# Order of tile conversions, k/v loads and stores at the end of the first unit's first stage

## The chip, the cores and the metric

The kernel runs on one core of a Trainium2 chip. The metric is the device time of one execution in microseconds (us). The core's engines each run their own instructions in order and wait for one another through semaphores. In the profile they are PE (TensorE, matrix products; PEld is its weight load), ACT (ScalarE), DVE (VectorE), POOL (GpSimd) and SP (SyncE, which here only issues transfers; its queue is shown as SPq). Transfers run on 16 DMA engines that all queues share.

## What is computed

A linear attention without softmax, normalized per head, followed by a feed-forward layer:

```python
kv = np.einsum('bhsd,bhse->bhde', k, v)
out = np.einsum('bhsd,bhde->bhse', q, kv)
rms = np.sqrt(np.mean(out * out, axis=-1, keepdims=True) + 1e-06)
x = (out / rms * g_norm).transpose(0, 2, 1, 3).reshape(4608, 512)
h = x @ w_in                      # (512, 2048)
g = s * np.maximum(h, 0.0) ** 2 + b
result = g @ w_out                # (2048, 512)
```

There are 8 batches of 8 heads, 576 positions and 64 columns per head. q, k, v and g_norm are float32; w_in and w_out are float64, and the chip has to turn them into float32 itself.

## The kernel before

**Units.** The 4608 rows are done in nine units of 512 rows. A unit has a first stage (x by w_in, then squared ReLU, scale s and offset b) and a second (by w_out). The first unit is special: during it the weights are loaded and converted.

**Products.** Most of both stages is computed by a scheme of seven products in place of eight (Strassen's, in Winograd's form), on halves of the operands. The products are called x1, z2, x6, y7, x5, x3 and y4: the letter is the PSUM tile (x_ps, z_ps, y_ps) that they go to, the digit the number of the product. x1, x6, x5 and x3 accumulate in one tile, and between them ScalarE copies the intermediate sum out: `keep("r1", ...)` behind x1, r2 behind x6, r4 behind x5 (line 718, shown as `r<-x_ps`). A product that continues in the tile must wait for the copy. The results are four tiles a11, a12, a21 and a22 for each of the four blocks s of the 2048 columns, and the sum s1 = a21 + a22.

In the first unit the blocks s = 0, 1, 2 are computed plainly (`mm1_plain`, twelve slots), and only the block s = 3 by seven products (`mm1`). Its x3 and y4 are put behind the first product of the second stage, x1(0), in the loop at line 1782. For a11, a12 and a22 VectorE adds the copy (line 250) and squares the ReLU (line 647), and `scale_g` later has ScalarE scale them (line 644). For a21 all of it is on ScalarE (lines 652, 653, 644).

**Weights.** w_in and w_out come in 16 tiles of 1 MB: tiles 0 to 7 are w_in, 8 to 11 the upper half of w_out (w_up), 12 to 15 the lower (w_dn). A tile is loaded into one of three buffers (tag "raw"). `raw(i)` is ScalarE's part of its conversion (lines 225 and 230, in place), `convert(i)` VectorE's (a shift, line 235, and an integer addition, line 245, into the final place); the end of convert(i) frees the buffer and sends the load of tile i + 3. `more(i)` subtracts halves of w_up for the seven products. When the tiles are through, the same three buffers take, in turn, k and v of batch 1, heads 0 to 3 (behind convert(13)), heads 4 to 7 (behind convert(14)), and a temporary (behind convert(15)).

**What the first unit also does.** `store_w2(1, 5)` writes two planes of w_up to DRAM, for the units after this one (four transfers on SP). `load_kv(1, i)` loads k and v (two transfers each on SP), `loads(1, half)` loads q for the second unit (four transfers each). `kv_product(1)` uses k and v in slot 6 of the second stage, and the attention for the second unit is spread over slots 7 to 13 as in `side_of`. Later stores (planes 3, 2, 6, 7 and 4) go out on the same queue; `t4` overwrites plane 2 of w_dn, and so waits for its store.

**Order.** The order of instructions on each engine is the order in which the program's lines are written. SP issues transfers in order too: one whose buffer is not free holds up all behind it. In `first_unit`, the loop over functions at line 1663 writes the order around x1 to x5; the loop at line 1782 that around the second stage.

Of the kernel before, what the change touches and what calls it, by code (L numbers as in the profile page):

```python
# [16 lines left out]
def kernel(  # L17
# [78 lines left out]
    def load_kv(b, i, pool, queues=(nc.sync,), **kw):  # L96

        t = pool.tile([P, 4 * R * D], U32, name="kv_sb", **kw)
        view = t.bitcast(FP32).rearrange("p (m l j d) -> p m l j d", m=2, l=2, j=R)
        for l in range(2):  # L100
            kv_in[b, 2 * i + l] = view[:, 0, l], view[:, 1, l]
        rows = P // len(queues)
        for m, src in enumerate((k, v)):
            flat = src[b, 4 * i : 4 * i + 4].rearrange("(l r) (p j) d -> (r p) l (j d)", l=2, j=R)
            for r, queue in enumerate(queues):
                at = slice(r * rows, r * rows + rows)
                queue.dma_start(
                    out=view[at, m].rearrange("p l j d -> p l (j d)"), in_=flat[at]
                )
# [73 lines left out]
    convp = tc.alloc_tile_pool(name="convp", bufs=1, side="right")  # L183
# [80 lines left out]
    def sums_w_in(s):  # L264
        ws[s] = wp.tile([P, 3, KH, 2, P], FP32, name=f"ws_{s}")
        a11, a12 = wa[s][:, :KH], wa[s][:, KH:]
        a21, a22 = wb[s][:, :KH], wb[s][:, KH:]
        s1, s2, s4 = (ws[s][:, i] for i in range(3))

        def s12():  # L270
            add(s1, a21, a22)
            sub(s2, s1, a11)

        def s34():
            sub(a21, a11, a21)
            sub(s4, a12, s2)

        return s12, s34
# [30 lines left out]
    def sub_w_out(i, a, b, steps=range(NS)):  # L309

        for s in steps:
            blocks = slice(2 * s, 2 * s + 2)
            sub(W2_AT[i][:, blocks], W2_AT[a][:, blocks], W2_AT[b][:, blocks])

    def store_w2(*which):
        for i in which:
            for q in range(2):
                nc.sync.dma_start(
                    out=w2_dram[i][:, q], in_=W2_AT[i][:, :, q * P : q * P + P]
                )  # L320
# [280 lines left out]
    def x_sums(u):  # L601
        b11, b12 = xT[u][:, :KH, :TB], xT[u][:, :KH, TB:]
        b21, b22 = xT[u][:, KH:, :TB], xT[u][:, KH:, TB:]

        def tiles(*which):
            for i in which:
                xs[u, i] = xp.tile([P, KH, TB], FP32, name=f"xs_{i}", tag=f"xs_{i}")

        def t12():
            tiles(5, 6)  # L610
            sub(xs[u, 5], b12, b11)
            sub(xs[u, 6], b22, xs[u, 5])

        def t34():
            tiles(7, 4)
            sub(xs[u, 7], b22, b12)
            sub(xs[u, 4], b21, xs[u, 6])

        return t12, t34
# [42 lines left out]
    def g_s1(s):  # L662
        add(ga["s1", s], ga["a21", s], ga["a22", s])
# [3 lines left out]
    def scale_g():  # L667
        while to_scale:
            affine(to_scale.pop(0))
# [831 lines left out]
    def hi(n, h=None):  # L1501
        fold_hi(blocks[n], h)

    def lo(n, h=None):
        round_lo(blocks[n], h)

    def shift(n, h=None):
        shift_hi(blocks[n], place(n), h)

    def plus(n, h=None):  # L1510
        add_lo(blocks[n], place(n), h)
        if h != 0:
            send_w()

    def more(n):

        s, lower = where(n)
        if n >= 2 * NS:
            if not lower:
                sub_w_out(5, 5, 1, [s])  # L1520
# [66 lines left out]
    def pairs_of(u):  # L1587
        return [attention_of_two(c) for c in (4 * u, 4 * u + 2)]
# [30 lines left out]
    def loads(u, i):  # L1619

        if u < U:
            for load in load_q(4 * u + 2 * i):
                load()  # L1623

    def raw(i):
        hi(i)
        lo(i)

    def convert(i):
        shift(i)  # L1630
        plus(i)

    def first_unit():
        of_x = x_sums(0)
        of_w = []

        for n, slot in enumerate(slots0):
            if n > 1:
                out_of = slot()
                if out_of:  # L1640
                    out_of()
                if n % 4 == 0:
                    g_s1(n // 4 - 1)
            if 0 < n < 9:
                raw(n + 2)
                convert(n + 2)
            elif n == 0:
                continue
            elif n == 9:
                of_w += sums_w_in(3)  # L1650
                of_w[0]()
            elif n == 10:
                of_x[0]()
                raw(11)
                of_x[1]()
            else:
                of_w[1]()
            if n < 11:
                scale_g()
            if n == 9:  # L1660
                more(8)
        a = mm1(0, NS - 1)
        for fn in (
            a["x1"], scale_g, partial(convert, 11), partial(more, 9),
            a["z2"], partial(raw, 12),
            a["x6"], scale_g, partial(g_s1, 2),
            a["y7"], partial(convert, 12),
            a["x5"], partial(raw, 13), scale_g, partial(more, 10), partial(more, 11),
        ):
            fn()  # L1670
        return a

    def x3(a):
        a["x3"]()

    def y4(a):
        for name in ("y4", "y4_square", "x3_s1", "x3_s3"):
            a[name]()
# [64 lines left out]
    for u in range(U):  # L1743
        A, B = pairs_of(u + 1) if u + 1 < U else (None, None)
        if u == 0:
            last = first_unit()
            second = mm2(0)
        else:
            if u == 1:
                loads(2, 0)  # L1750
                loads(2, 1)
            first, at_second = sides(u, A, B)
            if u > 1:
                run, last = mm1_deep(u)
                second = mm2(u, last, at_second)
                run(lambda n: [fn() for fn in first.get(n, [])], second["early"])
                second["rest"]()
                continue
            steps = [mm1(u, s) for s in range(NS)]
            second = mm2(u)  # L1760
        for s in range(NS if u > 0 else 0):
            a = steps[s]

            def at(n):
                for fn in first.get((s, n), []):
                    fn()

            at(0)
            a["x1"]()
            if s:  # L1770
                x3(steps[s - 1])
            a["z2"]()
            at(1)
            if s:
                y4(steps[s - 1])
            a["x6"]()
            at(2)
            a["y7"]()
            at(3)
            a["x5"]()  # L1780
        side = side_of(A, B, lambda: [fn() for fn in x_sums(u + 1)], u)
        for n, slot in enumerate(second):
            slot()
            if u == 0:
                if n == 0:
                    store_w2(1, 5)
                    for name in ("x3", "y4", "y4_square"):
                        last[name]()
                    convert(13)
                    scale_g()  # L1790
                    load_kv(1, 0, convp, tag="raw", bufs=3)
                    raw(14)
                    last["x3_s1"]()
                elif n == 1:
                    convert(14)
                    load_kv(1, 1, convp, tag="raw", bufs=3)
                    raw(15)
                    loads(1, 0)
                    loads(1, 1)
                elif n == 2:  # L1800
                    convert(15)
                    t2 = convp.tile([P, 4 * R * D], FP32, name="w_t2", tag="raw", bufs=3)
                    W2_AT[6] = t2[:, : FC // 2 * HN].rearrange("p (f n) -> p f n", n=HN)
                elif n == 4:
                    store_w2(3, 2)
                    sub_w_out(6, 3, 5)
                    store_w2(6)
            if n == 0 and u > 0:
                x3(steps[-1])
                y4(steps[-1])  # L1810
            for step in side.get(n, []):
                step()
        if u == 0:
            tc_late()
            pump()
# [30 lines left out]
```

## Time and profile before

| | us |
|---|---|
| median of 4 runs | 911.71 |
| lowest, highest | 910.71, 912.14 |
| the profiled execution | 911.80 |
| its span | 910.0 |
| TensorE busy | 897.2 |
| VectorE busy | 667.3 |
| ScalarE busy | 358.5 |

The granted clock of TensorE was 1.00 in the profiled execution. The span is the time from the first to the last instruction that the profile shows. A row of the timeline gives the start, the length, the engine, the source line, the operation, the tiles out<-in, and a count if rows were merged; in brackets stand the time in which the engine was idle before the row and what ended it. The queue's rows give the time SP took to issue a transfer, not the time until the data landed. The part of the span that the change touches lies between 70 and 95 us:

| us | DVE busy | ACT busy | DMA share | GB/s |
|---|---|---|---|---|
| 80 to 84 | 3.17 | 2.90 | 0.58 | 172 |
| 84 to 88 | 2.38 | 2.86 | 1.02 | 322 |
| 88 to 92 | 3.86 | 4.00 | 1.17 | 323 |
| 92 to 96 | 3.64 | 0.78 | 1.06 | 346 |

[...] PE is busy for the whole of each of these stretches.

### The profile page before, as it was taken

Reading aid. Unit: us, or ns where it says so; the run is one execution under the profiler, and the core shown is the slowest. Engines: PE = TensorE matmul, PEld = TensorE weight load, DVE = VectorE, ACT = ScalarE, POOL = GpSimd, SP = SyncE. Lnnn points to the kernel's source line nnn. Section 1 sums busy time; section 2 is a strip of 40 time slices with the busy share of each in tenths; the row PEclk is TensorE's granted clock in tenths of the full one; section 3 lists DMA queues with packets and bytes.
Section 4 is the critical chain, followed back from the end, with each engine's and each line's share of the span. In section 5 each row is a group of like instructions: output and inputs, shape, how many; then the busy total and the mean of one; then the engine's idle time right before and its main releaser. Section 6 shows DMA issues by size and latency. Waiting matters only on the chain.

```text
span 910.0 us, 19247 instructions
## 1 busy us (share of the span) xinstructions
PE 897.2 (99%) x7514; PEld 824.1 (91%) x7514; DVE 667.3 (73%) x1234; ACT 358.5 (39%) x603; POOL 228.3 (25%) x432
## 2 busy tenths in 40 slices
PE   7998999999999999999999999999999999999998
PEld 6887888888889998999889998999899989999998
DVE  2888677588557985887678857895878778874686
ACT  3877224531147115640366026701580057104710
POOL 2000016113624232810273035603440300021000
PEclk9999999999999999999999999999999999999999
DMA  9686957339953994379626973597439812891286
GB/s 260 221 291 198 266 157 229 106 80 380 347 142 77 277 336 141 78 229 309 214 70 178 293 254 94 123 306 257 133 88 287 289 35 56 276 303 49 57 256 185
DMA packets 120138, 180.34 MB, mean 198 GB/s; under 512 B 29168, under 2 KB 46320, under 8 KB 120048
## 3 DMA queue, kind: packets, MB, share of 16 engines
q1 hardware_dynamic: 101552, 153.00, 54.1%
q0 software_dynamic: 15040, 23.88, 9.0%
q10 hardware_dynamic: 3456, 2.23, 1.0%
q8 instruction: 60, 0.98, 0.5%
q14 instruction: 30, 0.25, 0.1%
HBM read 153.36 MB, written 25.69 MB: 197 GB/s over the span
## 4 chain that ended last, share of the span: by engine, by line
PE 89%; DVE 6%; DMA 3%; ACT 1%; issue 1%; SPq 0%; DVEq 0%; ACTq 0%
PE x_ps L91 46%; PE y_ps L91 25%; PE z_ps L91 9%; PE sx_ps L91 4%; PE y_ps L545 2%; DMA kv_sb<-in_v_dram 1%; PE kv_ps L366 1%; DMA w_raw<-in_moe_w_out_dram 1%; DMA w_raw<-in_moe_w_in_dram 1%; PE z_ps L366 1%; DVE xs L253 1%; DVE wb L245 0%; DVE xn L578 0%; DVE a L253 0%; PE y_ps L366 0%
## 5 line engine op out<-in xcount | busy, mean ns | idle before, releaser
L1623 POOL DMA_DIRECT2D q_sb<-in_q_dram x256 | 144.1, 571 | 136.3 <-ACT a L652 63.0
L1210 POOL DMA_DIRECT2D out_dram<-o x110 | 55.0, 506 | 397.6 <-issue 151.7
L91 PE MATMUL x_ps<-w_sb,sub 128*128 128x128 f32 x1176 | 148.8, 275 | 0.6 <-DVE r L250 0.6
L91 PEld LDWEIGHTS x_ps<-w_sb,sub 128*128 128x128 f32 x1176 | 139.7, 192 | 0.9 <-DVE r L250 0.9
L644 ACT ACTIVATE a<-a,b_col,s_col 128x512 f32<-128x512 f32 x144 | 116.5, 815 | 30.2 <-DVE a L647 24.2
L91 PE MATMUL x_ps<-xs,ws 128*128 128x256 f32 x528 | 125.4, 380 | 1.9 <-ACT r L718 1.8
L91 PE MATMUL y_ps<-xs,wb 128*128 128x256 f32 x528 | 124.6, 381 | 0.5 <-DVE wb L253 0.5
L91 PEld LDWEIGHTS x_ps<-xs,ws 128*128 128x128 f32 x528 | 96.7, 190 | 14.6 <-ACT r L718 3.1
L91 PEld LDWEIGHTS y_ps<-xs,wb 128*128 128x128 f32 x528 | 97.5, 190 | 13.6 <-PE x_ps L91 0.9
L819 ACT COPY a<-x_ps 128x512 f32<-128x512 f32 x28 | 16.4, 585 | 216.1 <-PE x_ps L91 216.0
L91 PE MATMUL x_ps<-xT,wa 128*128 128x256 f32 x360 | 83.7, 381 | 0.1
L91 PEld LDWEIGHTS x_ps<-xT,wa 128*128 128x128 f32 x360 | 66.8, 190 | 10.3 <-issue 1.5
L250 DVE TENSOR_TENSOR r<-sx_ps,a 128x256 f32<-128x256 f32 x63 | 26.6, 422 | 62.2 <-PE sx_ps L91 62.1
L91 PE MATMUL x_ps<-w_sb,a 128*128 128x128 f32 (+1 forms) x432 | 64.9, 298 | 0.0
L91 PE MATMUL y_ps<-w_sb,a 128*128 128x128 f32 (+1 forms) x416 | 62.1, 295 | 0.0
L91 PEld LDWEIGHTS x_ps<-w_sb,a 128*128 128x128 f32 x432 | 58.9, 191 | 3.3 <-issue 0.4
L91 PEld LDWEIGHTS y_ps<-w_sb,a 128*128 128x128 f32 x416 | 56.1, 192 | 2.1
L250 DVE TENSOR_TENSOR a<-y_ps,r 128x512 f32<-128x512 f32 x38 | 26.1, 688 | 39.9 <-PE y_ps L91 32.2
L250 DVE TENSOR_TENSOR r<-x_ps,o 128x256 f32<-128x256 f32 (+1 forms) x84 | 29.7, 354 | 29.3 <-PE x_ps L91 28.6
L91 PE MATMUL y_ps<-w_sb,sub 128*128 128x128 f32 x392 | 49.5, 275 | 0.0
L253 DVE TENSOR_TENSOR a<-a,a 128x512 f32<-128x512 f32 x72 | 46.8, 684 | 0.4
L91 PE MATMUL z_ps<-w_sb,a 128*128 128x128 f32 (+1 forms) x352 | 46.8, 280 | 0.0
(185 smaller groups left out, 1519.8 us busy)
## 6 DMA issues: line engine op xcount, KB each, us to landing
w_sb<-w SPq DMA_DIRECT2D x385, 256.0 KB, 4.6
w_raw<-in_moe_w_in_dram SPq DMA_DIRECT2D x8, 1024.0 KB, 7.0
w_raw<-in_moe_w_out_dram SPq DMA_DIRECT2D x8, 1024.0 KB, 7.5
w_sb<-w SPq DMA_DIRECT2D x14, 512.0 KB, 9.3
w<-sub POOLq DMA_DIRECT2D x28, 256.0 KB, 6.2
w_sb<-in_k_dram SPq DMA_DIRECT2D x24, 288.0 KB, 5.0
w_sb<-in_v_dram SPq DMA_DIRECT2D x24, 288.0 KB, 5.2
out_dram<-o POOLq DMA_DIRECT2D x92, 64.0 KB, 4.0
```

The lines of the kernel that those rows point to most:

```text
L91: nc.tensor.matmul(o, lhsT=lhsT, rhs=rhs, start=start, stop=stop, skip_group_check=True)
L250: nc.vector.tensor_tensor(out=o, in0=a, in1=b, op=ALU.add)
L253: nc.vector.tensor_tensor(out=o, in0=a, in1=b, op=ALU.subtract)
L366: nc.tensor.matmul(ps[r][(r ^ l) * HB : (r ^ l) * HB + HB, i, :], lhsT=kv[l][0][rows, j, :], rhs=kv[l][1][rows, j, :], start=(j == 0), sto ...
L545: nc.tensor.matmul(ps[l][32 * p : 32 * p + 32, r, lo:hi], lhsT=bd_kv[b % 2][rows, p, at : at + 32], rhs=st["qT"][rows, p, lo:hi], start=Tr ...
L644: nc.scalar.activation(t, t, AF.Identity, scale=s_col, bias=b_col)
L819: nc.scalar.copy(g_tile("a11", s), st["x", s])
L1210: queues[s % 2].dma_start(out=view[b, jj, :, cols], in_=st[name, j][s * w : s * w + w, cols])
L1623: load()
```

## The change

Two places of the first unit are reordered; no operation is added or left out.

```diff
             a["x1"], scale_g, partial(convert, 11), partial(more, 9),
-            a["z2"], partial(raw, 12),
-            a["x6"], scale_g, partial(g_s1, 2),
+            a["z2"],
+            a["x6"], partial(raw, 12), scale_g, partial(g_s1, 2),
             a["y7"], partial(convert, 12),
             a["x5"], partial(raw, 13), scale_g, partial(more, 10), partial(more, 11),
...
                 if n == 0:
+                    convert(13)
+                    load_kv(1, 0, convp, tag="raw", bufs=3)
                     store_w2(1, 5)
                     for name in ("x3", "y4", "y4_square"):
                         last[name]()
-                    convert(13)
+                    raw(14)
                     scale_g()
-                    load_kv(1, 0, convp, tag="raw", bufs=3)
-                    raw(14)
                     last["x3_s1"]()
```

On ScalarE, raw(12) moves behind the copy r2 of x6, and raw(14) ahead of the scaling of a12. On VectorE, convert(13) moves ahead of the addition and the square of a12. On SP, the load of k and v of heads 0 to 3 (two transfers) moves ahead of the four stores of planes 1 and 5. TensorE's and GpSimd's order is the same in both kernels.

## The prediction

> **What bounds the kernel now.** I read the page first: the busy line, then the chain that ended last over the whole span, then that chain in order of time for the first 230 us, then the timelines of TensorE, ScalarE, VectorE and SyncE's queue between 64 and 127 us.
>
> ```profile
> PE 897.2 (99%) x7514; PEld 824.1 (91%) x7514; DVE 667.3 (73%) x1234; ACT 358.5 (39%) x603; POOL 228.3 (25%) x432
> PE 89%; DVE 6%; DMA 3%; ACT 1%; issue 1%; SPq 0%; DVEq 0%; ACTq 0%
> ```
>
> TensorE (PE) sets the end. The change can only move it by making PE wait less or more. PE's timeline names every wait of it, and after the first 32 us there are five; three stand where the change is:
>
> ```profile
> 68.31 1.89 PE L91 MATMUL z_ps<-xT,wa 128*128 128x256 f32 x8
> 71.26 1.99 PE L91 MATMUL x_ps<-xs,ws 128*128 128x256 f32 x8 [1.06 <-ACT r L718]
> 73.75 1.97 PE L91 MATMUL y_ps<-xs,wb 128*128 128x256 f32 x8 [0.50 <-DVE wb L253]
> 76.51 1.99 PE L91 MATMUL x_ps<-xs,ws 128*128 128x256 f32 x8 [0.79 <-ACT r L718]
> 78.34 3.62 PE L91 MATMUL x_ps<-w_up,a 128*128 128x256 f32 x16
> ```
>
> The rows are z2, x6, y7, x5 and the start of the second stage. Each number in front is a start, the bracket the idle time and who ended it. ScalarE shows why x5 waited: r2 (the third row) stands behind the two activations of raw(12).
>
> ```profile
> 73.04 0.82 ACT L644 ACTIVATE a<-a,b_col,s_col 128x512 f32<-128x512 f32 x1 [1.84 <-DVE a L691]
> 73.76 1.17 ACT L225 ACTIVATE w_raw<-w_raw 128x1024 f32<-128x1024 f32 x1
> 74.83 1.17 ACT L230 ACTIVATE w_raw<-w_raw 128x1024 uint32<-128x1024 uint32 x1
> 75.87 0.58 ACT L718 COPY r<-x_ps 128x512 f32<-128x512 f32 x1
> 78.14 0.82 ACT L644 ACTIVATE a<-a,b_col,s_col 128x512 f32<-128x512 f32 x1 [1.69 <-DVE a L647]
> 78.86 0.57 ACT L718 COPY r<-x_ps 128x512 f32<-128x512 f32 x1
> ```
>
> **Step 1, raw(12) behind r2's copy.** Its two activations hold ScalarE from 73.76 to 75.87, 2.11 us. With them behind it, r2 starts at 73.76 (x6 ended before y7's wait, near 73.2) and is done near 74.3. A product of eight matmuls that starts after a wait takes 1.83 us from start to start (76.51 to 78.34), one without 1.73 (81.79 to 83.52). So y7 runs from 73.75 to 75.58, x5 to 77.31, and the second stage begins at 77.31 in place of 78.34: a gain of 1.03 us. The two other waits, x6's for r1 and y7's for VectorE's wb, have nothing of the change ahead of them, so they stay. raw(12) itself now ends near 76.35, before convert(12) starts at 78.63, and before the activation that waits for VectorE until 78.14; that gap of 1.69 us is its cover. Without it the 0.47 us by which raw(12) comes later would be paid.
>
> The Trainium skill (Perfetto Trace Analysis, Tensor Engine Instruction) says that a matmul's end in a profile is computed, not observed. By the modelled ends this step is worth the bracket, 0.79; by the starts, 1.03. I take the starts; the sum differs by 0.24.
>
> **Does the gain survive the next waits on PE?** Each start below is the old one less 1.03. The first product of stage two needs the scaled a11 in its last quarter: 77.31 + 12 x 0.216 = 79.9, and the activation from 78.14 ends at 78.96. x3 (80.76) needs r4's copy, done at 79.4. y4 (82.49) needs VectorE's a22 add, done at 81.3. x1(1) (84.21) needs its bank read by the Relu of a21: that starts at 83.08, behind the copy that starts at 82.76, and takes 0.63: done at 83.7. This is the tightest, 0.5 us. Past this, PE's rows run without a gap to 142.19 us.
>
> **Step 2, convert(13) ahead of the last readings.** VectorE's shift and add take 1.97 us (86.78 to 88.75).
>
> ```profile
> 81.92 1.29 DVE L253 TENSOR_TENSOR w_up<-w_up 128x512 f32<-128x512 f32 x2
> 85.44 0.69 DVE L250 TENSOR_TENSOR a<-y_ps,r 128x512 f32<-128x512 f32 x1 [2.24 <-PE y_ps L91]
> 86.17 0.69 DVE L647 SCALAR_TENSOR_TENSOR a<-a 128x512 f32<-128x512 f32 x1
> 86.78 0.69 DVE L235 TENSOR_SCALAR w_dn<-w_raw 128x1024 uint32<-128x1024 uint32 x1
> 87.61 1.23 DVE L245 CUSTOM_DVE_ANT_0 w_dn<-w_raw,w_dn 128x2048 uint16<-128x2048 uint16 x1
> ```
>
> VectorE sits idle for 2.24 us, and raw(13) is done at 81.55, so the conversion fits in: 83.2 to 85.2. The a12 add behind it could start at 84.4 with the earlier y4 and starts at 85.2, 0.8 late by that and 0.24 earlier than before. a12 is first needed by z2(0) near 94.6; nothing else waits. Cost 0; without that gap 1.97 of VectorE, still under the 6 us of slack a12 has. The sum s1 of step 3 comes by 87.1 and is wanted at 87.67 + 2.6 = 90.3.
>
> **Step 3, raw(14) ahead of scale_g.** Its 2.10 us (87.62 to 89.72) go to 85.1 to 87.2, behind a21's scaling, which ended at 85.01 + 0.82 and now ends 0.64 earlier. Tile 14 has landed: its load was issued at 76.2 and took 4.9. a12's scaling moves to 87.2 to 88.0, wanted at 94.6. convert(14) then ends near 89.1 (before: near 91.4), convert(15) near 91.7 (before 93.4). Cost 0.
>
> **Step 4, SyncE's queue.** Moved: two loads (k and v of heads 0 to 3, 576 KB each) past four stores of 512 KB.
>
> ```profile
> 80.70 0.37 SPq L200 DMA_DIRECT2D w_raw<-in_moe_w_out_dram  x1
> 81.12 7.16 SPq L318 DMA_DIRECT2D w<-w_up  x4
> 88.86 1.18 SPq L107 DMA_DIRECT2D kv_sb<-in_k_dram  x1
> 90.08 0.50 SPq L107 DMA_DIRECT2D kv_sb<-in_v_dram  x1
> 91.43 0.37 SPq L107 DMA_DIRECT2D kv_sb<-in_k_dram  x1
> 91.84 0.47 SPq L107 DMA_DIRECT2D kv_sb<-in_v_dram  x1
> ```
>
> Now the queue stops behind tile 15's load until convert(13) ends at 85.2; k and v go out at 85.2 to 86.9, the stores behind them at 86.9 to 94.1 (7.16 again) instead of 81.1, the second k and v at 94.1 to 95.0 instead of 91.4, then eight loads of q. The DMA engines were full without a break from 82.9 to about 99; tile 15 alone keeps them to about 85.3, and the first k needs some 1.5 us to start (tile 15: issued at 80.70, traffic up from 82.3). So some 1.5 us of traffic time is lost and everything behind is that much later. The last v landed at 102.4 (91.84 + 10.6); now 102.4 + 1.5 = 103.9 by traffic, or 95.0 + 10.6 = 105.6 by issue. kv_product starts at 106.06 - 1.03 = 105.03, and its second half, which alone reads the last v, 1.1 later, at 106.2. Cover 0.6 to 2.3. Cost: nothing at the low end, an estimate of 0.5 at the upper; I take 0.
>
> The Trainium skill (DMA: Bandwidth & Descriptors, Anatomy of one DMA) speaks against this step: a semaphore wait is held by the issuing sequencer, while the DMA engines just drain their queues. Its fit of 2 us plus bytes at 436 GB/s would land the last v at 95.0 + 3.4 = 98.4, with 8 us of cover; the measured 10.6 us under this traffic decides, and the step then stands at 0.6.
>
> Behind it the stores of w_dn's planes 3 and 2 go out 1.5 later (105.9), and VectorE's t4, which overwrites plane 2 at 115.22 - 1.03 = 114.2, must wait for them. Their landing is not shown for the last; by the one before it (113.05, plus one store at 290 GB/s, 1.8) about 114.9, now 116.4: VectorE would wait 2.2. Its next stretch has 1.98 us of idle time before 121.25 and 2.78 before 125.58, which take that up. Cost 0 to 0.3, taken 0.
>
> **The chain after 125 us** goes through VectorE, though PE is never more than 0.2 us late there: it starts with an add that waited 2.78 us for PE's x3(0), so it moves with PE. From 144 us to the end PE is again without gaps but two (0.2 and 0.4 us), whose sources move with it.
>
> **Sum.** Gains 1.03; losses 0 (bounds 0 to 0.8). The profiled execution took 911.80 with a span of 910.0; the span becomes 909.0, that execution 910.8. It stood 0.09 over the median of 911.71, so the median becomes 910.7, 0.11% less. A measurement of this kernel can tell about 0.2%, 1.8 us, from no change.
>
> **Rivals.**
> - A, slower: the queue. kv_product runs into the last v. It decides from a landing after 106.2, and is a net loss from 107.2. For: the ring in front of the DMA engines was already full, single stores took 3.33 us to issue, and the stores now go out behind 1.15 MB more. If all four take 3.33, the second k and v go out at 86.9 + 13.3 = 100.2, the last v lands at 111.3, PE waits 5.1, and the time is 911.7 + 4.1 = 915.8. With half of that delay (3.1 us on 105.6, a landing of 108.7), 913.2. Against: the traffic is the same bytes in another order, and by it the landing is 103.9. Chance 0.21 for beyond 913.5.
> - B, no effect: PE's gain is eaten where it was to be handed on, by x1(1)'s bank (0.5 of cover), k and v (0.6 at worst) or t4: 911.2 to 911.9. For: three thin covers. Chance 0.12.
> - C, more than I see: x6's and y7's waits shrink too. By starts, x6 is 71.26 - 70.04 = 1.22 late and y7 73.75 - 73.09 = 0.66; with all of it 911.7 - 2.9 = 908.8. Against: neither r1's copy nor wb's subtraction moves. Chance 0.15, some of it for what a shifted DMA does elsewhere.
>
> **How the numbers follow.** The forecast has 0.52, with a range of its own of 910.2 to 911.3. Forecast and B lie within 0.2% of the median (909.9 to 913.5): 0.64; C is faster, 0.15; A slower, 0.21. The range runs from 909.3 (part of the way to C) to 913.4 (A with half its delay) and leaves out about two in ten.
>
> **What would show it.** In the profile after: x5 straight behind y7 with no bracket, r2's copy near 73.8, raw(12) behind it; x6's and y7's brackets unchanged; stage two's first row at 77.3; convert(13) at 83.2 in the idle time; k and v issued at 85.2, the stores behind; kv_product near 105.0 with no DMA wait. A bracket at kv_product with in_v would mean A; PE's row of 142.19 not moved by 1.0 would mean B.

## The result, and the profile after

| | us |
|---|---|
| kernel before, median of 62 runs | 910.95 |
| changed kernel, median of 43 runs | 909.59 |
| ratio | 0.9986, 95% interval 0.9982 to 0.9991 |
| profiled execution after, its span | 909.28, 907.5 |

The change makes the kernel faster by 0.14%, 0.8 to 1.6 us by the interval; 1.03 was forecast. The median of before is 0.76 us lower here than the 911.71 of its first four runs, from which the forecast was counted. The two profiled executions differ by 2.5 us of span, more than the medians do (1.36). That difference matters below.

PE's timeline after, the rows that answer to those shown of before:

```profile
68.39 1.89 PE L91 MATMUL z_ps<-xT,wa 128*128 128x256 f32 x8
70.11 1.89 PE L91 MATMUL x_ps<-xs,ws 128*128 128x256 f32 x8
72.37 1.97 PE L91 MATMUL y_ps<-xs,wb 128*128 128x256 f32 x8 [0.36 <-DVE wb L253]
74.17 1.89 PE L91 MATMUL x_ps<-xs,ws 128*128 128x256 f32 x8
75.90 3.62 PE L91 MATMUL x_ps<-w_up,a 128*128 128x256 f32 x16
```

x5 (74.17) has no bracket any more and starts 1.80 us after y7, where before it was 76.51 - 73.75 = 2.76. But x6 (70.11) has lost its bracket of 1.06 too, and y7's has shrunk. Stage two starts 78.34 - 75.90 = 2.44 us earlier: 1.38 of it were already there at y7 (73.75 - 72.37), which nothing of the change stands ahead of, and 1.06 came between y7 and the start of stage two. ScalarE shows the swap:

```profile
71.66 0.81 ACT L644 ACTIVATE a<-a,b_col,s_col 128x512 f32<-128x512 f32 x1 [1.80 <-DVE a L691]
72.38 0.56 ACT L718 COPY r<-x_ps 128x512 f32<-128x512 f32 x1
72.84 1.18 ACT L225 ACTIVATE w_raw<-w_raw 128x1024 f32<-128x1024 f32 x1
73.91 1.15 ACT L230 ACTIVATE w_raw<-w_raw 128x1024 uint32<-128x1024 uint32 x1
76.76 0.81 ACT L644 ACTIVATE a<-a,b_col,s_col 128x512 f32<-128x512 f32 x1 [1.70 <-DVE a L647]
```

r2 (72.38) stands directly behind the scaling, raw(12) behind it, and the wait for VectorE that was to cover it is there (1.70). VectorE's timeline shows convert(13) in the third and fourth row (its shift and its addition), where before there was a gap of 2.24, and the a12 addition behind it:

```profile
79.93 0.69 DVE L647 SCALAR_TENSOR_TENSOR a<-a 128x512 f32<-128x512 f32 x1
80.54 1.28 DVE L253 TENSOR_TENSOR w_up<-w_up 128x512 f32<-128x512 f32 x2
81.74 0.69 DVE L235 TENSOR_SCALAR w_dn<-w_raw 128x1024 uint32<-128x1024 uint32 x1
82.56 1.23 DVE L245 CUSTOM_DVE_ANT_0 w_dn<-w_raw,w_dn 128x2048 uint16<-128x2048 uint16 x1
83.71 0.68 DVE L250 TENSOR_TENSOR a<-y_ps,r 128x512 f32<-128x512 f32 x1
```

SyncE's queue has the first k and v ahead of the four stores (the fifth and sixth row are the second k and v):

```profile
79.32 0.37 SPq L200 DMA_DIRECT2D w_raw<-in_moe_w_out_dram  x1
83.82 0.37 SPq L107 DMA_DIRECT2D kv_sb<-in_k_dram  x1
84.23 0.46 SPq L107 DMA_DIRECT2D kv_sb<-in_v_dram  x1
84.75 8.33 SPq L318 DMA_DIRECT2D w<-w_up  x4
93.18 1.33 SPq L107 DMA_DIRECT2D kv_sb<-in_k_dram  x1
94.56 0.51 SPq L107 DMA_DIRECT2D kv_sb<-in_v_dram  x1
```

The last v took 7.1 us to land: 101.7. kv_product starts at 103.62 without a bracket and reads it 1.1 later, so 3.0 us of cover (time to spare before a wait) were left.

### The profile page after: what moved, and what is told of

Its sections match the earlier page's. It is cut to its first block, busy times and chain, and to the rows that moved or that the text cites. A ratio compares the mean times of both kernels' runs of the same rounds, so it can differ in the third digit from the quotient of the medians.

```text
span 907.5 us, 19247 instructions
## 1 busy us (share of the span) xinstructions
PE 896.6 (99%) x7514; PEld 824.4 (91%) x7514; DVE 667.3 (74%) x1234; ACT 357.6 (39%) x603; POOL 227.6 (25%) x432
## 4 chain that ended last, share of the span: by engine, by line
PE 89%; DVE 6%; ACT 2%; DMA 2%; issue 1%; ACTq 0%; DVEq 0%
PE x_ps L91 46%; PE y_ps L91 26%; PE z_ps L91 9%; PE sx_ps L91 4%; PE y_ps L545 2%; DMA kv_sb<-in_v_dram 1%; PE kv_ps L366 1%; DMA w_raw<-in_moe_w_in_dram 1%; PE z_ps L366 1%; ACT w_raw L230 1%; DVE xs L253 1%; ACT w_raw L225 1%; DVE xn L578 0%; DVE a L253 0%; PE y_ps L366 0%
```

## The experiments

**1. The copy alone.** Only raw(12) moves; the second block is as before.

```diff
-            a["z2"], partial(raw, 12),
-            a["x6"], scale_g, partial(g_s1, 2),
+            a["z2"],
+            a["x6"], partial(raw, 12), scale_g, partial(g_s1, 2),
```

> Step 1 alone: raw(12) behind r2's copy, all else as before. Theory (the copy is the whole gain): 0.9 to 1.2 us under the kernel before, ratio near 0.9988; x5 follows y7 without a bracket, r2 stands directly behind the scaling row. Rival (the second block gives part of it): 0.3 us or less here. Rival (the profiled 2.4 us are the change's): 2 us or more here.

Measured: 909.43 against 910.42, ratio 0.9989 (0.9980 to 0.9998). x5 starts 1.73 us after y7. This is the size of the whole change.

**2. The second block alone.** raw(12) stays ahead of r2.

```diff
+                    convert(13)
+                    load_kv(1, 0, convp, tag="raw", bufs=3)
                     store_w2(1, 5)
...
-                    convert(13)
+                    raw(14)
                     scale_g()
-                    load_kv(1, 0, convp, tag="raw", bufs=3)
-                    raw(14)
```

> The second block alone: convert(13), the first load of k and v and raw(14) moved up, raw(12) left ahead of r2. Theory: no change, within 0.3 us of the kernel before (ratio 0.9997 to 1.0003), x5's bracket of about 0.8 back, kv_product without a wait for a transfer. Rival A (the queue costs time): slower, with a bracket of in_v at kv_product. Rival (the block helps by itself): 0.5 us or more faster.

Measured: 910.21 against 910.42, ratio 0.9996 (0.9988 to 1.0005): no change that can be told, though the interval alone would also allow a gain of 1.1 us. x5's bracket is back, at 0.50 (the third row; x6 and y7 stand ahead of it):

```profile
70.22 1.89 PE L91 MATMUL x_ps<-xs,ws 128*128 128x256 f32 x8
71.95 1.89 PE L91 MATMUL y_ps<-xs,wb 128*128 128x256 f32 x8
74.34 1.99 PE L91 MATMUL x_ps<-xs,ws 128*128 128x256 f32 x8 [0.50 <-ACT r L718]
```

The bracket is smaller than 0.8 because ScalarE was further ahead of TensorE here, and y7 had no wait of its own: raw(12) starts 0.33 us before y7 (71.62 against 71.95), in the first profile of before 0.01 after it. x5 is 0.66 late by starts (74.34 - 71.95 - 1.73). So the cost of raw(12) itself differs somewhat from one execution to the next. kv_product has no wait for a transfer, so rival A is out for this execution. From the start of stage two to the end of the span it needs 907.8 - 76.17 = 831.6 us, like the two profiles of before (831.7 each, the second in experiment 3), so this block gains nothing there either.

**3. The kernel before again**, unchanged.

> The kernel before, unchanged, for another profile of it. Theory (the 1.4 us that the profile after gained ahead of the change come from when the tiles of w_out land, which differs from one execution to the next): ratio 1.000, and the r1 copy, the y7 row and the landing of tiles 8 to 11 differ from the first profile by up to 1.5 us while the order is the same; x5's bracket stays 0.7 to 0.9. Rival (the change moves them): the first profile's starts are repeated within 0.2 us.

Measured: 910.40 against 910.42, ratio 0.9999 (0.9990 to 1.0008). Its profile differs from the first of the same kernel (x6, y7, x5 and the start of stage two):

```profile
70.10 1.89 PE L91 MATMUL x_ps<-xs,ws 128*128 128x256 f32 x8
72.26 1.96 PE L91 MATMUL y_ps<-xs,wb 128*128 128x256 f32 x8 [0.26 <-DVE wb L253]
74.98 2.00 PE L91 MATMUL x_ps<-xs,ws 128*128 128x256 f32 x8 [0.76 <-ACT r L718]
76.81 3.62 PE L91 MATMUL x_ps<-w_up,a 128*128 128x256 f32 x16
```

x6 runs without a wait, y7 is 1.49 us earlier than in the first profile with half its bracket, and only x5's bracket is as it was. So a difference of 1.38 us at y7 comes without the change; it belongs to the execution. Where it comes from is seen at the loads of tiles 8 to 10 (issued between 46 and 55 us): from issue to landing 7.6, 7.5 and 7.9 us in the first profile of before, 6.4, 5.1 and 4.9 here, 6.3, 5.5 and 5.1 in the profile after. ScalarE's waits for landing tiles of w_out, in the first profile of before:

```profile
54.27 1.14 ACT L225 ACTIVATE w_raw<-w_raw 128x1024 f32<-128x1024 f32 x1 [1.06 <-DMA w_raw<-in_moe_w_out_dram]
58.08 1.17 ACT L225 ACTIVATE w_raw<-w_raw 128x1024 f32<-128x1024 f32 x1 [0.92 <-DMA w_raw<-in_moe_w_out_dram]
61.81 1.16 ACT L225 ACTIVATE w_raw<-w_raw 128x1024 f32<-128x1024 f32 x1 [0.34 <-DMA w_raw<-in_moe_w_out_dram]
```

In the profile after, the same three activations start at 53.96, 56.77 and 60.02 without a bracket. With the late tiles ScalarE and VectorE come to raw(11) and to wb later (67.85 and 72.92 in the first profile of before, 66.46 and 71.54 in the profile after), and x6 and y7 wait for them.

**4. raw(11) behind its copy, too**, and the scaling of s = 2 behind raw(11), on top of the change.

```diff
                 of_x[0]()
-                raw(11)
                 of_x[1]()
...
-            if n < 11:
+            if n < 10:
                 scale_g()
...
-            a["x1"], scale_g, partial(convert, 11), partial(more, 9),
+            a["x1"], partial(raw, 11), scale_g, partial(convert, 11), partial(more, 9),
```

> The changed kernel with raw(11), too, behind its copy (r1 of x1), and the scaling of s = 2's a21 behind it. Theory (a copy that PE waits for must not stand behind a conversion): x6 follows z2 without a bracket, worth 0 to 1.2 us over the changed kernel by how late the tiles land, about 0.5 in the median: 1.3 to 2.2 us under the kernel before. Rival (VectorE sets the next start anyway): y7's bracket for wb grows by what x6's loses, and the time stays within 0.3 us of the changed kernel.

Measured: 909.67 against 910.42, ratio 0.9992 (0.9982 to 1.0002). x6 has no bracket, but the gain expected over the changed kernel is not there. The profile fell in an execution with early tiles (5.8, 4.9 and 5.1 us to land), in which x6 needs no help.

**5. All three waits treated.** raw(11) behind r1, the subtractions for wb ahead of the last plain block's reading, `more` and the scaling later.

```diff
                 of_x[0]()
-                raw(11)
                 of_x[1]()
+                of_w[1]()
-            else:
-                of_w[1]()
-            if n < 11:
+            if n < 10:
                 scale_g()
-            if n == 9:
-                more(8)
...
-            a["x1"], scale_g, partial(convert, 11), partial(more, 9),
-            a["z2"],
+            a["x1"], partial(raw, 11), partial(convert, 11),
+            a["z2"], partial(more, 8), partial(more, 9),
             a["x6"], partial(raw, 12), scale_g, partial(g_s1, 2),
```

> The changed kernel with all three waits of PE treated: raw(11) behind r1, the subtractions of wb and ws ahead of the last plain block's reading, more(8), more(9) and the scaling of s = 2 behind them. Theory (these brackets are all that this stretch of PE loses): x1, z2, x6, y7, x5 and stage two follow one another at 1.73 us each with no bracket, whatever the tiles' landing; 0.4 to 1 us under the changed kernel in the median, 1.6 to 2.3 under the kernel before (ratio 0.9975 to 0.9983), and a smaller spread of its runs. Rival (VectorE is the next limit): a bracket appears at the first product of stage two, for the a11 scaling or the conversion of tile 11, and the time is that of the changed kernel.

Measured: 909.02 against 910.56, ratio 0.9990 (0.9981 to 0.9999). The medians alone would give 0.9983, but the eleven runs fall into two groups, six from 908.65 to 909.02 and five from 909.92 to 911.16, and the median is the top of the lower one. Beside the changed kernel (909.87, experiment 8) it is 0.85 lower by the medians and 0.2 by the means. The brackets are gone; that the extra gain is there can't be told, and the spread is hardly smaller (2.5 us against 2.7). In the profile stage two starts at 75.27; in experiments 1 and 8, where none of x6, y7 and x5 waited, it starts at 75.27 and 75.18, so nothing was left to gain in this execution. The version was run again beside the changed kernel:

> The version with all copies first again, next to the changed kernel on one chip. Theory (x6's and y7's waits, which come with late tiles, still cost the changed kernel something in the median): 0.3 to 1 us under the changed kernel of this call, no bracket at x6, y7 and x5 in the profile. Rival (the spread of the times is made elsewhere): the two medians within 0.3 us, the spread of runs the same, 2 us or more.

> The changed kernel a third time, as the partner of the run beside it. Theory: ratio to the kernel before 0.998 to 0.9995; x5 1.73 to 1.83 us behind y7; x6's and y7's brackets between 0 and 1.1 each by how late tile 11 is read; the span less the start of stage two 831.4 to 831.8, as in the other profiles.

Measured: 909.31 with ratio 0.9988 (0.9979 to 0.9997), its partner 909.69 with 0.9992 (0.9983 to 1.0001). The medians lie 0.4 apart, inside both intervals, the means again 0.2. This time the profile caught late tiles (7.4, 7.1 and 7.6 us to land), and shows what becomes of the gain (the rows are x5, the first product of stage two x1(0), x3, y4 and x1(1)):

```profile
74.32 1.89 PE L91 MATMUL x_ps<-xs,ws 128*128 128x256 f32 x8
76.05 3.62 PE L91 MATMUL x_ps<-w_up,a 128*128 128x256 f32 x16
79.50 1.89 PE L91 MATMUL x_ps<-xT,ws 128*128 128x256 f32 x8
81.92 1.99 PE L91 MATMUL y_ps<-xs,wb 128*128 128x256 f32 x8 [0.53 <-DVE a L250]
84.25 3.72 PE L91 MATMUL x_ps<-w_up,a 128*128 128x256 f32 x16 [0.34 <-ACT a L652]
```

x5 starts 2.2 us and stage two 2.3 us earlier than in the profile of before with about as late tiles. Then y4 waits for VectorE's a22 addition, and x1(1) for ScalarE's Relu of a21: x1(1) would start at 76.05 + 3.45 + 2 x 1.73 = 82.96 and starts at 84.25, so 1.29 us are given back. VectorE has no gap from 66 to 83 us in this execution, and the Relu stands on ScalarE behind a scaling that waited 1.56 us for VectorE; so with late tiles VectorE is the next limit.

**6. k and v behind q**, to measure the cover of kv_product, on top of the change.

```diff
-                    load_kv(1, 1, convp, tag="raw", bufs=3)
                     raw(15)
                     loads(1, 0)
                     loads(1, 1)
+                    load_kv(1, 1, convp, tag="raw", bufs=3)
```

> The changed kernel with k and v of heads 4 to 7 behind the eight loads of q on SyncE's queue, to measure the cover of kv_product. Theory (the last v has some 3 us of cover, and what goes beyond it PE pays in full): the two are issued 8 us later, near 101 to 102, land near 108, kv_product has a bracket of 3 to 4.5 us for in_v, and the time is 2 to 3.5 us over the kernel before (ratio 1.002 to 1.004). Rival (slack behind kv_product takes it up): the bracket is there and the time is within 0.5 us of the changed kernel.

Measured: 913.18 against 910.56, ratio 1.0026 (1.0012 to 1.0039), with runs from 909.51 to 915.34, a wider spread than any other version's. The last v went out at 99.86 and landed 7.6 us later, at 107.5:

```profile
103.36 1.28 PE L366 MATMUL kv_ps<-kv_sb 64*64 64x64 f32 x72
107.64 1.28 PE L366 MATMUL kv_ps<-kv_sb 64*64 64x64 f32 x72 [3.00 <-DMA kv_sb<-in_v_dram]
108.85 3.72 PE L91 MATMUL x_ps<-w_t,a 128*128 128x256 f32 x16
```

The second half of kv_product waits 3.00 us. From the start of stage two to the end of the span this execution needs 910.5 - 75.64 = 834.9 us, 3.3 more than the profile after (907.5 - 75.90 = 831.6): nothing behind kv_product takes the wait up.

**7. The cost doubled:** raw(13), too, ahead of r2's copy, on top of the kernel before.

```diff
-            a["z2"], partial(raw, 12),
+            a["z2"], partial(raw, 12), partial(raw, 13),
...
-            a["x5"], partial(raw, 13), scale_g, partial(more, 10), partial(more, 11),
+            a["x5"], scale_g, partial(more, 10), partial(more, 11),
```

> The kernel before with raw(13), too, ahead of r2's copy: the suspected cost doubled. Theory (PE pays for each conversion ahead of the copy): r2 and x5 2.1 us later, x5's bracket 2.7 to 3.0, the time 1.9 to 2.2 us over the kernel before (ratio 1.0021 to 1.0024). Rival (ScalarE's gap behind takes it up, or VectorE sets stage two): less than 1 us.

Measured: 913.90 against 910.56, ratio 1.0034 (1.0021 to 1.0046): 3.1 us in place of 2. The bracket is as expected, the rest is not (the last row, x3, is cut off by the end of the view):

```profile
72.26 1.97 PE L91 MATMUL y_ps<-xs,wb 128*128 128x256 f32 x8
77.03 2.77 PE L91 MATMUL x_ps<-xs,ws 128*128 128x256 f32 x8 [2.80 <-ACT r L718]
79.59 4.57 PE L91 MATMUL x_ps<-w_up,a 128*128 128x256 f32 x16
84.00 1.24 PE L91 MATMUL x_ps<-xT,ws 128*128 128x256 f32 x5
```

x5 starts 2.05 us later than in experiment 3 (74.98), from an equal y7 (72.26 in both). But then x5 takes 2.56 from start to start in place of 1.83, and the first product of stage two 4.41 in place of 3.45: 1.69 us more. The stretches below (from and to in us, the length, then the busy time of PE, PEld, DVE, ACT and POOL with the number of instructions in brackets, the granted clock of PE, the DMA share and GB/s) say why:

```profile
77.00:78.00 1.00, 0.97 (x5) 0.87 (x6) 0.86 (x3) 0.69 (x1) 0.00 (x0) 1.00 0.98 406
78.00:79.00 1.00, 1.00 (x4) 0.82 (x3) 1.00 (x1) 0.00 (x0) 0.00 (x0) 0.55 0.99 406
79.00:80.00 1.00, 1.00 (x3) 0.75 (x3) 0.18 (x1) 0.11 (x1) 0.00 (x0) 0.50 0.04 16
80.00:81.00 1.00, 1.00 (x4) 0.80 (x3) 0.49 (x1) 0.47 (x1) 0.00 (x0) 0.50 0.41 29
81.00:82.00 1.00, 1.00 (x5) 0.86 (x4) 0.97 (x3) 0.04 (x1) 0.00 (x0) 0.74 0.82 270
82.00:83.00 1.00, 1.00 (x7) 0.87 (x6) 1.00 (x2) 0.77 (x1) 0.00 (x0) 1.00 0.99 373
```

The granted clock fell to half for some 3 us, from about 1 us after the long wait. Of that loss 0.2 is won back: from the start of x5 to the end of the span this execution needs 1.5 us more than experiment 3 (834.97 against 833.52). The other runs fit this: four of the five have a mean clock of 0.997 or 0.998 and took 913.61 to 914.57 us; the single run at 1.000 took 912.63, 2.07 over the median of before, which is the cost that was expected.

**8. The changed kernel again.**

> The changed kernel again, beside the others and for a second profile. Theory: 1.0 to 1.4 us under the kernel before (ratio 0.9985 to 0.9989); x5 starts 1.73 to 1.83 us after y7, against 2.4 to 2.8 where raw(12) stands first; the last v lands 2.5 us or more before the second half of kv_product.

Measured: 909.87 against 910.56, ratio 0.9992 (0.9983 to 1.0001), a little above what was expected; the interval holds 0.9986, and 1 as well. x5 starts 1.73 us after y7, and the last v is issued 2.1 us earlier than in the profile after.

The measure that depends least on how late the tiles land is the time from y7's start to x5's, one profile each:

| raw(12) and r2's copy | us |
|---|---|
| conversion first: before, experiments 3 and 2 | 2.76, 2.72, 2.39 |
| two conversions first: experiment 7 | 4.77 |
| copy first: the change (its profile, experiment 8, the changed kernel beside the second run of 5) | 1.80, 1.73, 1.80 |
| copy first: experiments 1, 4, 5 and the second run of 5 | 1.73, 1.80, 1.73, 1.80 |

From the start of stage two to the end of the span it is 831.4 to 831.7 us in both profiles of before, all three of the change, and those of experiments 1, 2, 4 and the first run of 5. What differs between these executions is made ahead of stage two. In the second run of 5 it is 833.0, by the 1.29 given back, in experiment 6 834.9.

## Why the prediction was right

**The sum.** The difference was right in size: 1.03 lies inside the measured 0.8 to 1.6. The time itself was not: 909.59 stands below the forecast's own 910.2 to 911.3. Of the 1.1 us by which it undercuts the 910.7, 0.76 is the median of before, taken from four runs that happened to lie high, and 0.33 the difference (1.36 against 1.03), which the interval can't tell from nothing. That it still lies inside the wide range, 0.3 above its low end, is luck: the range had been drawn down to there for rival C, waits of x6 and y7 that the change would shorten, and no experiment shows the change doing that. The least that can be told was put too high, at 1.8 us: with 62 and 43 runs the interval is 0.8 us wide.

**Step 1 (1.03 us for the copy).** Right. Alone it gives 0.9989, about 1.0 us, and in the profile after 1.06 between y7 and stage two. Two conversions ahead of the copy move x5 by another 2.05 us, one conversion being 2.11. What one costs follows how far ScalarE is ahead: 0.69 by starts in experiment 2 (y7 to stage two takes 4.22 there and 3.53 in the profile after), 1.06 in the first profile of before. Reading starts and not the modelled ends was the better choice: 0.79 falls 0.27 short of the 1.06 seen.

**The next waits on PE.** Right for the change: x1(1) follows without a bracket; the Relu of a21 starts at 81.62 and ScalarE's next row at 82.25, against 82.80 for x1(1), 0.55 of cover where 0.5 was worked out. The row of 142.19 stands at 139.75, 2.44 earlier, as much as stage two. The second run of experiment 5 shows that this cover and y4's are the next to go: they are the ones that PE ran into when it came another 1.3 us earlier against late tiles.

**Steps 2 and 3 (0).** Right: the conversion went into VectorE's gap, the a12 addition came 0.7 us after it could have (0.8 was worked out), and experiment 2 finds no cost in the time behind the start of stage two.

**Step 4 (0, with a cover of 0.6 to 2.3).** Right in its cost, too careful in its cover: the stores took 8.33 us to issue and not 7.16 (nor rival A's 13.3), but the last v then landed in 7.1 us and not 10.6, so 3.0 us were left. Taking over a landing time from another order of the queue was the error; the traffic's own estimate (1.5 us later than before) was nearer. The fit of the Trainium skill (DMA: Bandwidth & Descriptors, Anatomy of one DMA) that the prediction set beside it, 3.4 us, is stated there for transfers that GpSimd issues, so it did not apply to these loads on SyncE's queue. The wait of 2.2 us at t4 did not come either: its subtraction started at 112.97, 0.1 after the work ahead of it. Experiment 6 shows that the mechanism of rival A is real and its price full: 3.0 us of wait, 3.3 from stage two to the end.

**What is open.** x6's bracket and about half of y7's in the first profile of before came from that execution; the prediction treated them as the kernel's and expected them unchanged. That they vary was not needed for its sum, but a comparison of two profiles alone would have credited the change with 2.4 us. Whether the late tiles alone make the spread between runs (3.6 us before, 3.4 after) isn't settled: two profiles with late tiles, of before and of the version with all copies first, start stage two late or lose time just behind it, but that version spread nearly as widely as the changed kernel. Nor is it settled why the same loads land in some 5 or some 7.5 us.

## What to carry to other kernels

On an in-order engine, put the copy that TensorE waits for ahead of work that only has to be done sometime; the gain is the work's length, less the time by which the copy is then done before TensorE needs it. Here that left 1.03 of 2.11 us, while a second conversion, with no such time left, moved x5 by nearly its full length (2.05). Before a difference of two profiles is put down to a change, find the first row at which they part and ask whether the change stands ahead of it; a second profile of the old kernel answers it. When a stall is removed, look up which covers are thinnest behind it: they say how much of a further gain will arrive.

## What the runs showed of the hardware that was not expected

A wait of TensorE of 2.80 us by the modelled ends (experiment 7) was followed by about 3 us at a granted clock of 0.50, which made the doubled cost 3.1 us where 2 were expected. A wait of 3.00 us in experiment 6 was not: the clock stayed at 1.00 in every stretch of 1 us from 107 to 114 us. So the length of the wait alone does not decide.

The Trainium skill (TensorE: Matmul & The Clock Gate, Part 1: The HAM clock gate) says that the clock is at half after at least one idle window of about 3.4 us and back at full after about 3.4 us of sustained work, and that the window runs freely and does not start with the kernel. The half clock and its length of some 3 us agree with the rows. That a wait of 2.80 us, shorter than the window, is followed by it does not, and what sets it apart from the longer wait of 3.00 us is open.
